# Sketched attention feeding a squared-ReLU network on one core: compact q features, planned order of the engines and a shorter prologue

## The chip, the core and the metric

The kernel runs on one core of one Trainium2 chip. The metric is the device time of that core in microseconds (us), median of several executions. A core has four compute engines that matter here: PE multiplies matrices (its weight loads are listed apart as PEld), DVE works elementwise and shuffles or transposes inside blocks of 32 rows, ACT copies and applies functions, POOL does small setup work and copies. SP only issues transfers.

## The reference, cut to what matters

```python
batch, n_heads, seq, head_dim = (4, 4, 1088, 32)         # float32
r = 8                                                   # rows of S1 and S2

def phi(x):                                             # 8 x 8 = 64 features per head
    a = np.einsum('rd,bhsd->bhsr', S1, x)
    b = np.einsum('rd,bhsd->bhsr', S2, x)
    return np.einsum('bhsi,bhsj->bhsij', a, b).reshape(*x.shape[:-1], r * r)
q_p, k_p = (phi(q), phi(k))
kv  = np.einsum('bhsf,bhsd->bhfd', k_p, v)
z   = np.sum(k_p, axis=2)
num = np.einsum('bhsf,bhfd->bhsd', q_p, kv)
den = np.einsum('bhsf,bhf->bhs', q_p, z)[..., None] + 1e-06
x   = (num / den) as 4352 rows of 128                   # 4 batches x 1088 rows, 4 heads x 32
h   = np.maximum(x @ w_in, 0.0)                         # w_in  128 x 2048
out = h * h @ w_out                                     # w_out 2048 x 128
```

Both kernels cut a batch into three chunks of at most 384 rows (384, 384, 320), and the 2048 hidden columns into 16 steps of 128. One FFN step is one f16 matmul `pg` (x times `w_in`), a Relu on ACT, a square, and one float32 matmul `po` (the square times `w_out`). There are 4 x 3 x 16 = 192 such steps.

## The kernel before

The q features need, for 4 heads x 64 features = 256 products, both factors spread over 256 rows. The kernel before lets PE do the spreading: the weights `sqa` and `sqb` hold each row of S1 and S2 eight times over. A matmul uses only 64 rows of the array, those of two heads, so there are two of each kind per group of columns:

```python
for c0 in range(0, S, 512):
    for pr in range(2):
        pa = psa.tile([128, 512], F32, tag="feat")
        nc.tensor.matmul(pa[:, 0:n], sqa[64*pr : 64*pr+64, :], qT[64*pr : 64*pr+64, c0 : c0+n])
        sa = wpool.tile([128, 512], F32, tag="sa")
        nc.scalar.copy(sa[:, 0:n], pa[:, 0:n])
        pb = psa.tile([128, 512], F32, tag="feat")
        nc.tensor.matmul(pb[:, 0:n], sqb[64*pr : 64*pr+64, :], qT[64*pr : 64*pr+64, c0 : c0+n])
        nc.vector.tensor_tensor(out=qp[...], in0=pb[:, 0:n], in1=sa[:, 0:n], op=mult)
    yield
```

The other matmuls of attention are `kf` (k features), `kvp` (k features times v with a column of ones) and `nd` (q features times `kvp`: numerator and denominator). The main loop runs all of batch 0's attention first, then the FFN of each batch with a stage of the next batch's attention at every fourth step. The order of instructions on each engine is left to a scheduler, which sees this program order:

```python
att = attn_gen(0)
for i, _ in enumerate(att): ...                  # the whole attention of batch 0
for b in range(B):
    issue_loads(b + 1); nxt = attn_gen(b + 1)    # (if there is a next batch)
    for t0, t1 in CHUNKS:
        for i, _ in enumerate(ffn_gen(b, t0, t1)):   # pg, Relu, square, po of one step
            if i % 4 == 2:
                next(nxt, None)
```

Of the kernel before, what the change touches and what calls it, by code (L numbers as in the profile page):

```python
# [9 lines left out]
F32 = mybir.dt.float32  # L10
# [10 lines left out]

@with_exitstack
def kernel(
# [13 lines left out]
    B, H, S, D = 4, 4, 1088, 32  # L37
    G = S // 32
    DFF = 2048
    NFF = DFF // 128  # L40
    NT = (S + 127) // 128
    TW = [min(128, S - 128 * t) for t in range(NT)]
    CHUNKS = [(0, 3), (3, 6), (6, 9)]
# [5 lines left out]
    Relu = mybir.ActivationFunctionType.Relu  # L49
    Copy = mybir.ActivationFunctionType.Copy  # L50
# [4 lines left out]
    fpool = ctx.enter_context(tc.tile_pool(name="ffn", bufs=4))  # L55
    psf = ctx.enter_context(tc.tile_pool(name="psf", bufs=3, space=bass.MemoryType.PSUM))
    psa = ctx.enter_context(tc.tile_pool(name="psa", bufs=2, space=bass.MemoryType.PSUM))


    s_nat = cpool.tile([128, 32], F32)  # L60
    nc.gpsimd.memset(s_nat[:], 0.0)
    for h in range(H):
        nc.sync.dma_start(s_nat[32 * h : 32 * h + 8, :], S1[:, :])
        nc.scalar.dma_start(s_nat[32 * h + 8 : 32 * h + 16, :], S2[:, :])

    def load_qk(dst, src, b, eng):
        eng.dma_start(
            dst[:, :],
            bass.AP(src.tensor, src.offset + b * H * S * D, [[G * D, 128], [1, G * D]]),
        )  # L70

    def load_v(dst, b):

        for g4 in range(4):
            for h in range(H):
                n = (G - g4 + 3) // 4
                nc.sync.dma_start(
                    _ap(dst, 32 * g4, 32, 33 * h, [[4 * 33, n], [1, 32]]),
                    bass.AP(
                        v.tensor,  # L80
                        v.offset + ((b * H + h) * S + g4) * D,
                        [[G * D, 32], [4 * D, n], [1, D]],
                    ),
                )

    loaded = {}

    def issue_loads(b):
        kn = bpool.tile([128, S], F32, tag="kn")
        qn = bpool.tile([128, S], F32, tag="qn")  # L90
        va = bpool.tile([128, NT * H * 33], F32, tag="va")
        load_qk(kn, k, b, nc.sync)
        nc.gpsimd.memset(_ap(va, 0, 128, 32, [[33, NT * H]]), 1.0)
        load_v(va, b)
        load_qk(qn, q, b, nc.scalar if b == 0 else nc.sync)
        loaded[b] = (kn, qn, va)

    issue_loads(0)

    w_in32 = cpool.tile([128, DFF], F32)  # L100
    nc.sync.dma_start(w_in32[:], moe_w_in[:, :])
    w_in = cpool.tile([128, DFF], F16)
    w_o = cpool.tile([128, DFF], F32)
    nc.sync.dma_start(
        _ap(w_o, 0, 128, 0, [[128, NFF], [1, 128]]),
        bass.AP(
            moe_w_out.tensor, moe_w_out.offset, [[128, 128], [128 * 128, NFF], [1, 128]]
        ),
    )

    iden = cpool.tile([128, 128], F32)
    make_identity(nc, iden[:])
    iden16 = cpool.tile([128, 128], F16)
    nc.gpsimd.tensor_copy(iden16[:], iden[:])

    s_T = cpool.tile([128, 32], F32)
    nc.vector.transpose(s_T[:, :], s_nat[:, :])
    sk = cpool.tile([128, 64], F32)
    sqa = cpool.tile([128, 128], F32)
    sqb = cpool.tile([128, 128], F32)  # L120
    nc.gpsimd.memset(sk[:], 0.0)
    nc.gpsimd.memset(sqa[:], 0.0)
    nc.gpsimd.memset(sqb[:], 0.0)
    for h in range(H):
        nc.vector.tensor_copy(  # L125
            sk[32 * h : 32 * h + 32, 16 * h : 16 * h + 16], s_T[32 * h : 32 * h + 32, 0:16]
        )
    for h in range(H):
        c = 64 * (h % 2)
        nc.vector.tensor_copy(  # L130
            _ap(sqa, 32 * h, 32, c, [[8, 8], [1, 8]]),
            _ap(s_T, 32 * h, 32, 0, [[1, 8], [0, 8]]),
        )
        nc.vector.tensor_copy(
            _ap(sqb, 32 * h, 32, c, [[8, 8], [1, 8]]),
            _ap(s_T, 32 * h, 32, 8, [[0, 8], [1, 8]]),
        )


    kvs = []  # L140
    for i in range(2):
        kv = cpool.tile([128, 2 * 66], F32, tag=f"kv{i}")
        nc.gpsimd.memset(kv[:], 0.0)
        kvs.append(kv)

    xT = {}
    betas = {}

    def attn_gen(b):
        kn, qn, va = loaded[b]  # L150
        kT = bpool.tile([128, S], F32, tag="kT", bufs=1)
        qT = bpool.tile([128, S], F32, tag="qT", bufs=1)
        qp = bpool.tile([128, 2 * S], F32, tag="qp", bufs=2)
        kv_sb = kvs[b % 2]
        xTb = bpool.tile([128, S], F16, tag="xT")
        beta = bpool.tile([128, NT], F32, tag="beta")
        xT[b], betas[b] = xTb, beta
        for c0, c1 in ((0, 512), (512, S)):
            nc.vector.transpose(kT[:, c0:c1], kn[:, c0:c1])  # L159
        yield  # L160
        for c0, c1 in ((0, 512), (512, S)):
            nc.vector.transpose(qT[:, c0:c1], qn[:, c0:c1])  # L162
        yield

        kvp = psa.tile([128, 2 * 66], F32, tag="acc", bufs=1)
        for t0 in range(0, NT, 3):
            kf = psa.tile([128, 3 * 64], F32, tag="feat")
            for i in range(3):
                w = TW[t0 + i]
                nc.tensor.matmul(  # L170
                    kf[0:w, 64 * i : 64 * i + 64],
                    kT[:, 128 * (t0 + i) : 128 * (t0 + i) + w],
                    sk[:, :],
                )
            fb = wpool.tile([128, 3 * 32], F32, tag="fb")
            kp = wpool.tile([128, 3 * 256], F32, tag="kp")
            segs = [(128, 3)] if TW[t0 + 2] == 128 else [(128, 2), (TW[t0 + 2], 1)]
            i0 = 0
            for w, n in segs:
                nc.scalar.copy(  # L180
                    _ap(fb, 0, w, 32 * i0, [[8, 4 * n], [1, 8]]),
                    _ap(kf, 0, w, 64 * i0 + 8, [[16, 4 * n], [1, 8]]),
                )
                i0 += n
            for i in range(3):
                w = TW[t0 + i]
                nc.vector.tensor_tensor(  # L187
                    out=_ap(kp, 0, w, 256 * i, [[64, 4], [8, 8], [1, 8]]),
                    in0=_ap(kf, 0, w, 64 * i, [[16, 4], [1, 8], [0, 8]]),
                    in1=_ap(fb, 0, w, 32 * i, [[8, 4], [0, 8], [1, 8]]),  # L190
                    op=mult,
                )
            for i in range(3):
                t = t0 + i
                w = TW[t]
                for pr in range(2):
                    nc.tensor.matmul(  # L197
                        kvp[:, 66 * pr : 66 * pr + 66],
                        _ap(kp, 0, w, 256 * i + 128 * pr, [[1, 128]]),
                        _ap(va, 0, w, t * H * 33 + 66 * pr, [[1, 66]]),  # L200
                        start=(t == 0 and pr == 0),
                        stop=(t == NT - 1),
                        skip_group_check=True,
                    )
            yield
        for h2 in range(2):
            nc.scalar.copy(
                _ap(kv_sb, 64 * h2, 64, 33 * h2, [[66, 2], [1, 33]]),
                _ap(kvp, 64 * h2, 64, 33 * h2, [[66, 2], [1, 33]]),
            )  # L210

        for c0 in range(0, S, 512):
            n = min(512, S - c0)
            pas, pbs = [], []
            for pr in range(2):
                pa = psa.tile([128, 512], F32, tag="feat")
                nc.tensor.matmul(  # L217
                    pa[:, 0:n], sqa[64 * pr : 64 * pr + 64, :], qT[64 * pr : 64 * pr + 64, c0 : c0 + n]
                )
                pas.append(pa)  # L220
                sa = wpool.tile([128, 512], F32, tag="sa")
                nc.scalar.copy(sa[:, 0:n], pa[:, 0:n])  # L222
                pb = psa.tile([128, 512], F32, tag="feat")
                nc.tensor.matmul(  # L224
                    pb[:, 0:n], sqb[64 * pr : 64 * pr + 64, :], qT[64 * pr : 64 * pr + 64, c0 : c0 + n]
                )
                nc.vector.tensor_tensor(  # L227
                    out=qp[:, pr * S + c0 : pr * S + c0 + n],
                    in0=pb[:, 0:n],
                    in1=sa[:, 0:n],  # L230
                    op=mult,
                )
            yield

        for t0, t1 in CHUNKS:
            nd = psa.tile([128, 3 * 132], F32, tag="acc", bufs=1)
            for t in range(t0, t1):
                w = TW[t]
                for pr in range(2):
                    o = 132 * (t - t0) + 66 * pr  # L240
# [162 lines left out]
```

## Time and profile before

Median 288.25 us of three runs (287.9 to 290.56); profiled span 286.6 us. I cut the span where ACT starts copying the last chunk of a batch out of `po` (tile `oT`), because at that point the batch's last `po` matmul is done.

| Stage | us | PE busy in it |
|---|---|---|
| start to first `pg` matmul | 53.29 | 37.9 |
| first `pg` to the end of batch 0 | 64.49 | 64.1 |
| batch 1 | 59.38 | 58.4 |
| batch 2 | 59.59 | 58.2 |
| batch 3 (FFN alone) | 43.53 | 41.4 |
| output of the last chunk | 6.32 | 0.6 |

The first fence is from the profile page of the kernel before: busy time with the share of the span and the number of instructions; the busy tenths of PE and the granted PE clock in 40 equal slices; the chain of waits by engine; two groups of instructions (busy us, mean ns, then idle time before them and what ended it).

```profile
PE 260.4 (91%) x1104; PEld 157.9 (55%) x1104; DVE 153.9 (54%) x441; ACT 114.2 (40%) x302; POOL 2.2 (1%) x17
...
PE   0578996999999999999989999999899999999991
...
PEclk9999999999999999999999999999999999999997
...
PE 86%; DVE 4%; ACT 3%; DMA 3%; issue 2%; ACTq 0%; DVEq 0%
...
L224 PE MATMUL pb<-qT,sqb 64*128 64x512 f32 (+1 forms) x48 | 25.2, 610 | 3.7 <-DVE qp L227 2.0
L217 PE MATMUL pa<-qT,sqa 64*128 64x512 f32 (+1 forms) x48 | 25.7, 621 | 0.9 <-DVE qp L227 0.9
```

PE is the limit: 91% busy, and 86% of the chain.

A float32 matmul is recorded as two passes ("x2"). In the prologue a pair `pa`, `sa`, `pb`, `qp` runs one after the other, 5.6 us from 14.86 to 20.45, and a `pa` takes 2.02 us where it takes 1.05 in the middle of the kernel. PE is at half speed there, although the clock row says 9 throughout.

### The profile page before, as it was taken

How to read it: one execution, taken by the hardware profiler on the slowest of the kernel's cores; microseconds unless marked ns; L12 is line 12 of the kernel's file. 1: busy time of each engine (PE TensorE's matmuls, PEld its weight loads, DVE VectorE, ACT ScalarE, POOL GpSimd, SP SyncE). 2: the span in 40 equal slices, each digit the busy share in tenths (PEclk: the TensorE clock that was granted, in tenths of full speed). 3: DMA queues.
4: the chain of work that ended last, by engine and by line, in shares of the span. 5: the costliest groups of instructions: out<-in, count | busy, mean ns of one | idle time of the engine just before them, and what ended most of it. 6: DMA issues, size and time to landing. Idle time of an engine off the chain costs nothing.

```text
span 286.6 us, 3493 instructions
## 1 busy us (share of the span) xinstructions
PE 260.4 (91%) x1104; PEld 157.9 (55%) x1104; DVE 153.9 (54%) x441; ACT 114.2 (40%) x302; POOL 2.2 (1%) x17
## 2 busy tenths in 40 slices
PE   0578996999999999999989999999899999999991
PEld 0422765856743578677434687765346664444550
DVE  0810106569634587937346788655345784653550
ACT  0211040423534363546434645436344445463541
POOL 2000000000000000000000000000000000000000
PEclk9999999999999999999999999999999999999997
DMA  4486520000037022000000000000000000000000
GB/s 156 64 285 155 177 41 8 0 0 0 3 77 199 0 57 70 0 25 1 27 0 0 26 4 1 24 1 29 0 0 3 27 1 22 3 29 0 22 6 23
DMA packets 24889, 11.23 MB, mean 39 GB/s; under 512 B 18856, under 2 KB 23208, under 8 KB 24744
## 3 DMA queue, kind: packets, MB, share of 16 engines
q1 hardware_dynamic: 24664, 10.46, 14.1%
q10 hardware_dynamic: 208, 0.56, 0.5%
q8 instruction: 8, 0.13, 0.2%
q14 instruction: 9, 0.07, 0.1%
HBM read 8.79 MB, written 2.23 MB: 38 GB/s over the span
## 4 chain that ended last, share of the span: by engine, by line
PE 86%; DVE 4%; ACT 3%; DMA 3%; issue 2%; ACTq 0%; DVEq 0%
PE po L322 43%; PE pg L315 10%; PE pb L224 7%; PE kvp L197 7%; PE nd L241 7%; PE pa L217 6%; PE kf L170 4%; ACT gt L320 2%; DMA kn<-in_k_dram 2%; PE op L337 2%; DVE qp L227 1%; PE xp L300 1%; ACT oT L331 0%; ACT sa L222 0%; DMA s_nat<-in_S_dram 0%
## 5 line engine op out<-in xcount | busy, mean ns | idle before, releaser
L320 ACT ACTIVATE gt<-pg 128x384 f32<-128x384 f32 (+1 forms) x192 | 78.2, 480 | 70.3 <-PE pg L315 68.2
L315 PE MATMUL pg<-xTb,w_in 128*128 128x384 f16 (+1 forms) x192 | 47.4, 323 | 2.6 <-ACT gt L320 2.1
L315 PEld LDWEIGHTS <-w_in 128*128 128x128 f16 x192 | 19.6, 107 | 23.1 <-issue 15.3
L227 DVE TENSOR_TENSOR qp<-pb,sa 128x512 f32<-128x512 f32 (+1 forms) x24 | 12.7, 531 | 34.6 <-PE pb L224 24.7
L224 PE MATMUL pb<-qT,sqb 64*128 64x512 f32 (+1 forms) x48 | 25.2, 610 | 3.7 <-DVE qp L227 2.0
L217 PE MATMUL pa<-qT,sqa 64*128 64x512 f32 (+1 forms) x48 | 25.7, 621 | 0.9 <-DVE qp L227 0.9
L197 PEld LDWEIGHTS kvp<-va,kp 128*128 128x128 f32 (+1 forms) x144 | 22.0, 225 | 6.3 <-issue 5.5
L222 ACT COPY sa<-pa 128x512 f32<-128x512 f32 (+1 forms) x24 | 11.1, 461 | 35.3 <-PE pa L217 33.1
L170 PE MATMUL kf<-sk,kT 128*128 128x64 f32 (+1 forms) x72 | 13.8, 334 | 12.4 <-DVE sk L125 10.3
L197 PE MATMUL kvp<-va,kp 128*128 128x66 f32 (+1 forms) x144 | 23.1, 309 | 0.0
L241 PE MATMUL nd<-kv,qp 128*128 128x66 f32 (+1 forms) x144 | 22.1, 294 | 0.0
L241 PEld LDWEIGHTS nd<-kv,qp 128*128 128x128 f32 (+1 forms) x144 | 20.2, 208 | 2.8 <-issue 1.5
L170 PEld LDWEIGHTS kf<-sk,kT 128*128 128x128 f32 (+1 forms) x72 | 12.9, 250 | 13.9 <-issue 13.1
L224 PEld LDWEIGHTS pb<-qT,sqb 64*128 64x128 f32 x48 | 8.6, 217 | 15.4 <-DVE qp L227 5.5
L187 DVE TENSOR_TENSOR kp<-kf,fb 128x256 f32<-128x256 f32 (+1 forms) x36 | 13.2, 411 | 6.4 <-PE kvp L197 5.1
L217 PEld LDWEIGHTS pa<-qT,sqa 64*128 64x128 f32 x48 | 8.3, 215 | 8.6 <-issue 5.6
L306 ACT COPY xTb<-xp 128x384 f16<-128x384 f16 (+1 forms) x12 | 5.5, 462 | 16.5 <-PE xp L300 16.1
L341 ACT ACTIVATE ob<-op,beta 128x128 f32<-128x128 f32 (+1 forms) x36 | 10.7, 379 | 2.9 <-PE op L337 2.9
L331 ACT COPY oT<-po 128x384 f32<-128x384 f32 (+1 forms) x12 | 5.5, 462 | 15.4 <-PE po L322 15.4
L258 DVE TENSOR_SCALAR den<-nd 128x12 f32<-128x12 f32 (+2 forms) x16 | 2.6, 161 | 16.3 <-PE nd L241 16.3
L159 DVE STREAM_TRANSPOSE kT<-kn 128x512 f32<-128x512 f32 (+1 forms) x8 | 5.6, 721 | 6.6 <-DMA kn<-in_k_dram 6.6
L162 DVE STREAM_TRANSPOSE qT<-qn 128x512 f32<-128x512 f32 (+1 forms) x8 | 5.6, 722 | 3.8 <-PE pb L224 3.8
(640 smaller groups left out, 387.2 us busy)
## 6 DMA issues: line engine op xcount, KB each, us to landing
kn<-in_k_dram SPq DMA_DIRECT2D x4, 544.0 KB
out_dram<-ob SPq DMA_DIRECT2D x32, 64.0 KB
qn<-in_q_dram SPq DMA_DIRECT2D x3, 544.0 KB
va<-in_v_dram SPq DMA_DIRECT2D x32, 36.0 KB
va<-in_v_dram SPq DMA_DIRECT2D x32, 32.0 KB
w_in_105<-in_moe_w_in_dram SPq DMA_DIRECT2D x1, 1024.0 KB
qn<-in_q_dram ACTq DMA_DIRECT2D x1, 544.0 KB
out_dram<-ob SPq DMA_DIRECT2D x4, 32.0 KB
```

The costliest lines, as they stand in the source:

```text
L170: nc.tensor.matmul(kf[0:w, 64 * i : 64 * i + 64], kT[:, 128 * (t0 + i) : 128 * (t0 + i) + w], sk[:, :],)
L187: nc.vector.tensor_tensor(out=_ap(kp, 0, w, 256 * i, [[64, 4], [8, 8], [1, 8]]), in0=_ap(kf, 0, w, 64 * i, [[16, 4], [1, 8], [0, 8]]), in1 ...
L197: nc.tensor.matmul(kvp[:, 66 * pr : 66 * pr + 66], _ap(kp, 0, w, 256 * i + 128 * pr, [[1, 128]]), _ap(va, 0, w, t * H * 33 + 66 * pr, [[1, ...
L217: nc.tensor.matmul(pa[:, 0:n], sqa[64 * pr : 64 * pr + 64, :], qT[64 * pr : 64 * pr + 64, c0 : c0 + n])
L222: nc.scalar.copy(sa[:, 0:n], pa[:, 0:n])
L224: nc.tensor.matmul(pb[:, 0:n], sqb[64 * pr : 64 * pr + 64, :], qT[64 * pr : 64 * pr + 64, c0 : c0 + n])
L227: nc.vector.tensor_tensor(out=qp[:, pr * S + c0 : pr * S + c0 + n], in0=pb[:, 0:n], in1=sa[:, 0:n], op=mult,)
L241: nc.tensor.matmul(nd[0:w, o : o + 66], qp[:, pr * S + 128 * t : pr * S + 128 * t + w], kv_sb[:, 66 * pr : 66 * pr + 66],)
L315: nc.tensor.matmul(pg[:, 0:n], w_in[:, 128 * c : 128 * c + 128], xT[b][:, c0 : c0 + n])
L320: nc.scalar.activation(gt[:, 0:n], pg[:, 0:n], Relu)
L322: nc.tensor.matmul(po[:, 0:n], w_o[:, 128 * c : 128 * c + 128], g2[:, 0:n], start=(c == 0), stop=(c == NFF - 1),)
L341: nc.scalar.activation(ob[0:w, o : o + 128], op[0:w, o : o + 128], Copy, bias=0.0, scale=betas[b][0:w, t : t + 1],)
```

## The change

Its intent is to take work from PE in the middle, to start the FFN earlier, and to fix the order of every engine by a plan:

1. **Compact q features.** One matmul `qc` gives the 16 projections of each head once (64 of 128 rows used, one 32-row block per head). DVE shuffles rows inside the 32-row blocks to make the factors: one shuffle for `qb`, two for `qa`. So 256 features become two halves of all four heads, `kvp` and `nd` become 132 columns wide instead of 66, and a mask takes out products across heads.
2. **Order.** The scheduler is switched off. A small planner assigns each attention task to an FFN step, from a table of durations. The `pg` of a step is issued 3 steps ahead of its `po`. A square goes to ACT when the plan has ACT less loaded than DVE (76 of 192, the number by which ACT's instructions differ in the experiment squares_dve; I had counted 78 beforehand; none of them in the last batch, which has no attention to plan for).
3. **Short prologue.** Only batch 0's first chunk is made before the FFN. Its q features use replicated weights (three matmuls `rep`, no shuffles). Loads come in parts, `kf` of all tiles goes first, 8 idle matmuls keep PE active while the first x is made.

The diff replaces nearly the whole body. Its core, with cuts:

```diff
+    ctx.enter_context(tc.manual_schedule())
...
-                    kvp[:, 66 * pr : 66 * pr + 66],
-                    _ap(kp, 0, w, 256 * i + 128 * pr, [[1, 128]]),
-                    _ap(va, 0, w, t * H * 33 + 66 * pr, [[1, 66]]),
...
+                kvp[:, 132 * e : 132 * e + 132],
+                kp[:, 256 * (t % 4) + 128 * e : 256 * (t % 4) + 128 * e + 128],
+                va[b % 2][:, 132 * t : 132 * t + 132],
...
+            out=kvz[:, :], in0=st[b, "kvp"][:, 0 : E * 132], in1=hmask[:, :], op=mult
...
-                nc.tensor.matmul(
-                    pa[:, 0:n], sqa[64 * pr : 64 * pr + 64, :], qT[64 * pr : 64 * pr + 64, c0 : c0 + n]
-                )
...
+        nc.tensor.matmul(qc[:, 0:384], sq[:, :], qT[:, 384 * ch : 384 * ch + 384])
...
+        nc.vector.stream_shuffle(in_=st[b, "qc", ch][:, 0:384], out=qb[:, :], mask=mask_b)
...
+        nc.vector.stream_shuffle(in_=st[b, "qc", ch][:, 0:384], out=qa[:, :], mask=mask_a[e])
...
+        if sq_on_act:
+            nc.scalar.activation(g2[:, 0:n], gt[:, 0:n], Square)
+        else:
+            nc.vector.tensor_tensor(out=g2[:, 0:n], in0=gt[:, 0:n], in1=gt[:, 0:n], op=mult)
...
+    P = _Plan(NS + 4, {"PE": 0.95, "DVE": 1.2, "ACT": 0.6, "POOL": 9.0, "SP": 9.0})
...
+    for i in range(NS + 4):
+        if i + LA < NS:
+            ffn1(i + LA, act_square(i + LA))     # pg, Relu, square, LA = 3 steps ahead
+        if i < NS:
+            ffn2(i)                              # po
+        for f, args in P.slots[i]:               # the attention tasks planned for this step
+            f(*args)
```

(The comments are mine. `e` counts the two halves of the features, `b` batches, `ch` chunks.)

## The prediction

> **What bounds the kernel now.** The page: span 286.6 us (timed median 288.25), PE busy 91%, DVE 54%, ACT 40%; 86% of the chain of waits is PE. The timeline and the chain show three stages.
>
> 1. Prologue, 0 to 53.3 us, where the first `pg` matmul starts. PE waits for loads and batch-0 features, and its passes run at half speed: `kvp` takes 0.22 us a pass at 28 us, 0.108 at 183 us. The PEclk row shows 9 throughout, so it hides this. The Trainium skill ("TensorE: Matmul & The Clock Gate", Part 1) describes such a cold clock; the trace agrees.
> 2. Middle: the chain repeats every 59.38 us per batch (88.55, 147.93, 207.31), PE 98% busy: PE throughput.
> 3. Last batch, 232 to 280.3 us: 48.3 us for FFN alone, worth 38.4 by the steps below: `po` waits for DVE squares, `pg` for ACT Relus: latency, from issue order.
>
> **PE cost, start to start in the timeline.** FFN step: `po` 0.646 + `pg` 0.163 = 0.81 us (0.68 at 320 columns): 36.75 us per batch, unchanged. Kv and nd matmuls become 132 columns wide instead of 66, but at 0.108 us a pass they look weight-load-bound (an f16 load measures 107 ns); I estimate 0.113 us a pass, 4.1 us each group, nearly free. `pa`+`pb` (about 8.5 us per batch: 1.05 and 0.86 us per two passes of 512 columns, plus the rests) become three 384-column `qc`, 1.95 us: 6.5 us saved. Period: 36.75 + kf 2 + kv 4.1 + qc 1.95 + nd 4.1 + transposes 2.1 = 51 us.
>
> **DVE and ACT.** Added: nine shuffles per batch. The skill ("VectorE: DVE Perf Modes", perf-mode tier table) gives the shuffle only the 1x program; the 128x512 transpose takes 0.69 us here, so I estimate 0.55 us for 384 columns. No shuffle is in this trace. 78 of 192 squares go to ACT (about 0.45 us each). Summing the planned tasks at traced durations over the FFN part: PE 194.5 us, DVE 123, ACT 128, and PE is largest in every group of eight steps. So PE stays the limit; the added DVE work is off the critical path.
>
> **Prologue after.** Estimate: k half lands at 4 us, kf 5.5 (cold, 0.5 each) to 10, rep to 12.5, kv to 17 or 20 (warm or cold), kvz, nd to about 21, small DVE chain 2.4, transposes and copy 1.2: first `pg` at 24.5 us. The rest of batch 0 (4 us of PE) moves into FFN.
>
> **Sum.** 24.5 + 1 (fill) + 194.5 + 4 stalls + 5.5 tail = 229.5 span; plus 1.65 outside it and a little for the unexpected: 232 us, range 224 to 243. Sources: prologue about 25 us net, `pa`/`pb` 20, last batch 10.
>
> Chances: faster by over 2%: 0.98; within 2%: 0.01; slower: 0.01.
>
> **What would show it.** First `pg` at 22 to 28 us. Period 51 to 53 us. `qc` 0.65 us start to start; nd and kv passes at most 0.12 us; shuffles about 0.55 us. Last batch 38.5 us. DVE and ACT both near 60%.
>
> **What would make it wrong.** Kv/nd passes well over 0.113 us; hand order stalling PE because `po` or `nd` waits for DVE behind attention work; only two `pg` buffers with ACT doing Relu and square; PE cold through the prologue or re-throttled at its end; POOL copies holding up DVE; w_in landing late.

## More of the kernel before

`pa` and `pb` together have 51 us of busy time, but a mean over the span hides that they cost twice as much early as later. The chain in order of time (start, duration, what) shows the early ones:

```profile
14.86 2.02 PE pa L217 x2
...
16.89 0.59 ACT sa L222
...
17.62 2.05 PE pb L224 x2
...
19.70 0.70 DVE qp L227
...
20.45 2.08 PE pa L217 x2
...
28.12 5.74 PE kvp L197 x26
```

The stages, from the windows of the trace (stretch and length; then busy us and count of PE, PEld, DVE, ACT, POOL; granted clock; DMA share; GB/s):

```profile
0.00:53.29 53.29, 37.88 (x117) 25.09 (x118) 15.48 (x47) 8.09 (x17) 2.00 (x16) 1.00 0.45 119
...
117.78:177.16 59.38, 58.38 (x279) 36.17 (x277) 37.61 (x108) 27.59 (x75) 0.00 (x0) 1.00 0.04 10
...
236.75:280.28 43.53, 41.35 (x150) 22.05 (x148) 22.18 (x48) 21.30 (x58) 0.00 (x0) 1.00 0.05 13
```

In batch 1 PE has work 98% of the time and DVE 63%: a middle batch is paid in PE work. The last batch has no attention beside it and still takes 43.5 us.

## The result, and the profile after

The kernel after takes 227.03 us (median of 4 runs, 226.17 to 227.38) beside 288.62 us for the kernel before (4 runs, 287.9 to 290.56). The ratio is 0.7853, with a 95% interval of 0.7807 to 0.79. Here and below, a ratio is the mean time of one kernel's fast runs over the mean of the other's fast runs in the same rounds, so it is not quite the ratio of the medians quoted. The profiled execution is one of the four, 227.35 us, with a span of 225.6 us.

The page of the kernel after:

```profile
PE 209.5 (93%) x1044; PEld 144.0 (64%) x1044; DVE 142.0 (63%) x371; ACT 149.2 (66%) x359; POOL 12.2 (5%) x47
...
PE   0896899989999999999999999999999999999990
...
PEclk9999699999999999999999999999999999999996
...
PE 50%; issue 40%; ACT 3%; DVE 2%; DMA 1%; POOL 1%; POOLq 0%; ACTq 0%; DVEq 0%
...
L325 PE MATMUL nd<-kvz,qp 128*128 128x132 f32 x144 | 20.1, 277 | 0.6 <-DVE kvz L292 0.6
...
L309 DVE STREAM_SHUFFLE qa<-qc 128x384 f32<-128x384 f32 x22 | 11.9, 590 | 0.0
...
L299 PE MATMUL qc<-qT,sq 128*128 128x384 f32 x22 | 8.9, 486 | 0.0
```

PE lost 51 us of busy time and is still the fullest engine. `pa` and `pb`, 51 us, gave way to `qc`, 8.9 us (and 2 us of `rep`). The `nd` matmuls, twice as wide, take 20.1 us of busy time, less than the 22.1 they had, of which a part ran at half speed. Do not read the chain's "issue 40%" as a wait: the last output transfer is issued by POOL, which had nothing else to do for 89.7 us, and the chain follows that idle queue back. The chain's early part is sound:

```profile
6.66 3.98 PE kf L249 x18
10.64 1.97 PE rep L530 x6
12.60 4.06 PE kvp L281 x36
...
17.25 1.63 PE nd L325 x12
...
20.60 0.60 DVE sc L365
...
24.51 1.38 PE po L434 x2
...
29.13 0.65 PE po L434 x2
```

`kf` runs at 0.22 us a pass of 96 columns and `rep` right behind it at 0.33 us a pass of 384. In the middle 384 columns also take 0.33 us, so PE came to full speed within the first 4 us of its work. The stages from the windows, same columns as before:

```profile
0.00:22.74 22.74, 13.89 (x85) 11.68 (x86) 11.80 (x33) 6.62 (x14) 7.52 (x40) 1.00 0.81 229
22.74:80.52 57.78, 56.50 (x289) 39.52 (x289) 37.83 (x114) 42.38 (x101) 1.53 (x3) 0.97 0.14 41
80.52:131.55 51.03, 50.78 (x263) 35.33 (x262) 33.90 (x91) 37.66 (x93) 2.33 (x3) 1.00 0.15 45
131.55:181.83 50.28, 50.28 (x260) 35.32 (x259) 33.50 (x89) 37.33 (x91) 0.00 (x0) 1.00 0.04 12
181.83:218.95 37.12, 37.09 (x150) 21.76 (x148) 24.30 (x46) 24.11 (x57) 0.00 (x0) 1.00 0.05 16
...
22.74:28.30 5.56, 5.08 (x13) 2.50 (x13) 3.15 (x10) 4.18 (x9) 0.00 (x0) 0.69 0.12 46
```

Where the 61.0 us of span went (before minus after):

| Stage | before | after | gain |
|---|---|---|---|
| start to first `pg` | 53.29 | 22.74 | 30.6 |
| first `pg` to the end of batch 0 | 64.49 | 57.78 | 6.7 |
| batch 1 | 59.38 | 51.03 | 8.4 |
| batch 2 | 59.59 | 50.28 | 9.3 |
| batch 3 | 43.53 | 37.12 | 6.4 |
| output of the last chunk | 6.32 | 6.65 | -0.3 |

Batch 0's FFN stage gains less than the others because it took over the attention of chunks 1 and 2, about 4 us of PE by the prediction's estimate, and because PE's clock fell to 0.69 in its first 5.6 us (last line of the fence). A `po` matmul took 1.38 us there instead of 0.65.

How much PE time a batch needs, read from the PE timeline of a middle batch (from the start of each group of matmuls to the start of the next, summed by kind, us):

| | `po` | `pg` | `kf` | `kvp` | `nd` | q features | sum |
|---|---|---|---|---|---|---|---|
| before (117.78 to 177.16) | 30.98 | 7.71 | 1.81 | 4.12 | 3.99 | 8.75 | 57.4 |
| after (131.55 to 181.83) | 28.65 | 7.37 | 1.93 | 4.08 | 4.05 | 1.93 | 48.0 |

(The rest is small: transposes of about 1.6 us, and gaps.) So of some 9 us per batch, 6.8 come from the q features, and about 2.7 stand against `po` and `pg`. The latter is no less work. I put it down to waits that end in them and to what a change of array shape costs (see the experiments before_hand2 and before_hand3); it was not taken apart.

### The profile page after: what moved, and what is told of

Its sections match the earlier page's. It is cut to its first block, busy times and chain, and to the rows that moved or that the text cites. A ratio compares the mean times of both kernels' runs of the same rounds, so it can differ in the third digit from the quotient of the medians.

```text
span 225.6 us, 3224 instructions
## 1 busy us (share of the span) xinstructions
PE 209.5 (93%) x1044; PEld 144.0 (64%) x1044; DVE 142.0 (63%) x371; ACT 149.2 (66%) x359; POOL 12.2 (5%) x47
## 4 chain that ended last, share of the span: by engine, by line
PE 50%; issue 40%; ACT 3%; DVE 2%; DMA 1%; POOL 1%; POOLq 0%; ACTq 0%; DVEq 0%
PE po L434 24%; PE pg L415 7%; PE nd L325 6%; PE kvp L281 5%; PE kf L249 3%; PE qc L299 2%; ACT gt L422 1%; DMA s_nat<-in_S_dram 1%; PE op L453 1%; PE rep L530 1%; POOL sr L201 1%; PE xp L395 1%; ACT xT L404 1%; POOLq L681 0%; POOL va_116 L228 0%
## 5 line engine op out<-in xcount | busy, mean ns | idle before, releaser
L422 ACT ACTIVATE gt<-pg 128x384 f32<-128x384 f32 (+1 forms) x192 | 89.8, 470 | 49.5 <-PE pg L415 48.7
L415 PE MATMUL pg<-xT,w_in 128*128 128x384 f16 (+1 forms) x192 | 61.2, 319 | 1.0 <-ACT xT L404 0.6
L325 PEld LDWEIGHTS nd<-kvz,qp 128*128 128x128 f32 x144 | 19.6, 190 | 5.0 <-DVE kvz L292 0.8
L325 PE MATMUL nd<-kvz,qp 128*128 128x132 f32 x144 | 20.1, 277 | 0.6 <-DVE kvz L292 0.6
L249 PE MATMUL kf<-sk,kT 128*128 128x96 f32 x72 | 11.2, 306 | 6.7 <-POOL sr L201 6.7
L249 PEld LDWEIGHTS kf<-sk,kT 128*128 128x128 f32 x72 | 11.3, 225 | 9.0 <-POOL sr L201 6.6
L281 PEld LDWEIGHTS kvp<-va_116,kp 128*128 128x128 f32 x72 | 10.7, 190 | 4.2
L267 DVE TENSOR_TENSOR kp<-fs 128x1024 f32<-128x1024 f32 (+1 forms) x12 | 11.4, 953 | 2.4 <-ACT fs L260 2.4
L309 DVE STREAM_SHUFFLE qa<-qc 128x384 f32<-128x384 f32 x22 | 11.9, 590 | 0.0
L281 PE MATMUL kvp<-va_116,kp 128*128 128x132 f32 x72 | 11.1, 277 | 0.0
L281 PEld LDWEIGHTS kvp<-va_113,kp 128*128 128x128 f32 x72 | 9.6, 190 | 2.4
L281 PE MATMUL kvp<-va_113,kp 128*128 128x132 f32 x72 | 9.8, 276 | 0.0
```

The costliest lines, as they stand in the source:

```text
L249: nc.tensor.matmul(kf[:, 96 * i : 96 * i + 96], kT[:, 128 * (t0 + i) : 128 * (t0 + i) + 128], sk[:, :])
L267: nc.vector.tensor_tensor(out=_ap(kp, 0, 128, 0, [[32, 8 * n], [8, 4], [1, 8]]), in0=_ap(fs, 0, 128, 0, [[4, 8 * n], [1, 4], [0, 8]]), in1 ...
L281: nc.tensor.matmul(kvp[:, 132 * e : 132 * e + 132], kp[:, 256 * (t % 4) + 128 * e : 256 * (t % 4) + 128 * e + 128], va[b % 2][:, 132 * t : ...
L309: nc.vector.stream_shuffle(in_=st[b, "qc", ch][:, 0:384], out=qa[:, :], mask=mask_a[e])
L325: nc.tensor.matmul(nd[:, 132 * o : 132 * o + 132], st[b, "qp", ch, e][:, 128 * o : 128 * o + 128], st[b, "kvz"][:, 132 * e : 132 * e + 132 ...
L415: nc.tensor.matmul(pg[:, 0:n], w_in[:, 128 * c : 128 * c + 128], st[b, "xT"][:, 384 * ch : 384 * ch + n],)
```

## The experiments

My theory after the result: the gain is PE work taken away plus an earlier start, and the new DVE work lies in PE's shadow. The rivals: fixing the order by hand is itself worth most of the middle's gain; the shuffles on DVE hold PE back, so that replicated matmuls would do as well; the replicated first features and the idle matmuls are what makes the prologue short. An expectation states what each theory would give; where it names a theory by a letter or a short word, its numbers tell which of these is meant. All kernels gave correct results.

### auto_order: the same program with the scheduler on

```diff
-    ctx.enter_context(tc.manual_schedule())
```

> The changed kernel with the hand order switched off, so that the automatic scheduler may reorder (one line removed). Theory A (the gain is PE work and program structure; the emission order already holds the pipelining, and the compiled PE order hardly differs): within 1% of the changed kernel, 225 to 230 us. Rival B (the gain is the fixed order itself): at least 10 us longer, 237 us or more.

Measured: 224.73 us (224.11 to 225.44), ratio 0.7793 (0.7752 to 0.7833), a little under the 225 to 230 us of theory A. It is not slower than the kernel after; the medians differ by 2.3 us in its favour, and the intervals of the two ratios just overlap. Its first `pg` comes later (24.65 us), but the first chunk is done at 42.14 us instead of 44.23, since the scheduler placed more of chunk 1's attention ahead of the first `pg`. Batches 1, 2 and 3 are the same within 0.5 us (50.6, 50.3, 37.1). So switching the scheduler off is worth nothing; the program order that the planner writes is enough for it.

### before_hand: the old arithmetic in a hand order

The main loop is rewritten as the change has it: `pg` 3 steps ahead of `po`, one stage of attention after each step (with more, shorter stages), scheduler off.

```diff
+    ctx.enter_context(tc.manual_schedule())
+    LA = 3
...
+    for i in range(LA):
+        ffn1(i)
+    for i in range(NS):
...
+        if i + LA < NS:
+            ffn1(i + LA)
+        ffn2(i)
...
+        next(nxt, None)
```

> The kernel before, its arithmetic untouched, but ordered by hand: pg issued 3 steps ahead of po, one small attention stage after each FFN step, scheduler off. Theory A: the middle period falls only from 59.4 to 57.5-58.5 us (its PE work), the last batch from 43.5 to about 37.5 us; with the prologue about as long as before, 273 to 284 us in all. Rival B: most of the 61 us comes from order, 250 us or less.

Measured: 316.69 us (315.47 to 317.29), ratio 1.0975 (1.0918 to 1.1032). This is a plain miss: I expected a gain and got a loss of 28 us. The first `pg` came at 65.7 us (12.4 later than before), batches 1 and 2 took 65.6 and 68.5 us instead of 59.4 and 59.6; only the last batch became shorter, 39.1 instead of 43.5. A hand order of the old operations is not by itself an improvement. Why the middle lost 6 to 9 us is the subject of before_hand2 and before_hand3.

### before_compact: the new arithmetic alone

The kernel before, with its scheduler, its loads and its prologue, but with `qc`, shuffles, 132-column `kvp` and `nd`, and the mask.

```diff
-                    pa[:, 0:n], sqa[64 * pr : 64 * pr + 64, :], qT[64 * pr : 64 * pr + 64, c0 : c0 + n]
...
+            nc.tensor.matmul(qc[:, 0:n], sq[:, :], qT[:, c0 : c0 + n])
+            qb = wpool.tile([128, 512], F32, tag="qb")
+            nc.vector.stream_shuffle(in_=qc[:, 0:n], out=qb[:, 0:n], mask=mask_b)
+            for pr in range(E):
+                qa = wpool.tile([128, 512], F32, tag="sa")
+                nc.vector.stream_shuffle(in_=qc[:, 0:n], out=qa[:, 0:n], mask=mask_a[pr])
```

> The kernel before with only the compact q features: one qc matmul, shuffles, 132-wide kv and nd, mask; automatic order and old prologue kept. Theory A: middle period 59.4 minus 6.5 = about 53 us, first batch shorter by 5 to 12 us, total 255 to 265 us. Rival B: under 8 us gained, 280 us or more.

Measured: 254.44 us (253.11 to 255.91), ratio 0.8823 (0.876 to 0.8887), just under the 255 to 265 us expected. This one part of the change brings 33.8 of the 61 us. The stages:

| Stage | before | before_compact | after |
|---|---|---|---|
| start to first `pg` | 53.29 | 39.67 | 22.74 |
| first `pg` to the end of batch 0 | 64.49 | 58.13 | 57.78 |
| batch 1 | 59.38 | 52.76 | 51.03 |
| batch 2 | 59.59 | 53.23 | 50.28 |
| batch 3 | 43.53 | 43.65 | 37.12 |

The three stages with attention in them gain 6.4, 6.6 and 6.4 us, which is the 6.8 us of PE work from the table above. The surprise is the first row. The compact features shorten even the old prologue by 13.6 us, where the `pa`, `sa`, `pb`, `qp` pairs ran one at a time and at half speed. Part of it is PE's speed: here the 36 passes of `kvp` take 6.62 us, 0.184 a pass on average, so PE left half speed for a time in the prologue, while in the kernel before it stayed there until about 58 us (a `po` takes 1.28 us at 56.48 and 0.65 at 58.72). In the chain of before_compact, what is left of the prologue is issue of loads, a load of `kn`, and a single run of `kvp` (the last line is from PE's timeline):

```profile
7.62 0.45 SPq L77
8.11 0.46 SPq L77
...
16.13 7.35 DMA kn<-in_k_dram
23.48 0.67 PE qc L214 x2
24.16 6.62 PE kvp L200 x36
...
19.32 2.07 PE L214 MATMUL qc<-qT,sq 128*128 128x512 f32 x2 [2.07 <-DVE qa L219]
```

That load of `kn` belongs to batch 1, and `qc` of batch 0 does not read it, so I do not trust this link of the chain. In PE's timeline PE is idle for 2.07 us before the second `qc`, until DVE has made the factors from the first, and for 2.07 us again before the third (at 23.47 us), just after DVE's next shuffles. So here, unlike in the middle, the shuffles seem to hold PE up.

Line 77 issues the v loads, 16 for a batch, at 0.5 us from one issue to the next. The kernel after needs 10 transfers for v, and its `kvp` run starts at 12.60 us; that the number of transfers makes this difference is not shown. The last batch did not move at all: it has no q features.

### replicate_all: the same plan, but PE spreads the q features

Batches 1 to 3 use three replicated matmuls per chunk in place of `qc` and three shuffles. The planner's limit for PE had to be raised for it to find room.

```diff
-    P = _Plan(NS + 4, {"PE": 0.95, "DVE": 1.2, "ACT": 0.6, "POOL": 9.0, "SP": 9.0})
+    P = _Plan(NS + 4, {"PE": 1.2, "DVE": 1.2, "ACT": 0.6, "POOL": 9.0, "SP": 9.0})
...
+                P.add(("qr", b, ch), "PE", 0.65, after, r_q, b, ch, 2, first=first)
+                P.add(("qb", b, ch), "ACT", 0.46, [("qr", b, ch)], r_qb, b, ch)
...
+                    P.add(("qa", b, ch, e), "PE", 0.65, [prev], r_q, b, ch, e)
```

> The changed kernel with batches 1 to 3 using replicated-feature matmuls (3 of 0.646 us per chunk instead of 1) and no shuffles: PE work up 9 x 1.29 = 11.6 us, DVE down about 9 us. Theory A (PE is the limit, shuffles hidden): 11.6 us longer, 236 to 242 us. Rival C (the shuffles on DVE are what holds the PE): unchanged or shorter, 222 to 230 us.

Measured: 238.35 us (238.2 to 238.47), ratio 0.8264 (0.8218 to 0.831): 11.3 us more than the kernel after. The added PE work is 3 batches x 3 chunks x 2 matmuls x 0.65 us = 11.7 us. Nearly all of it shows, although DVE has 27 shuffles fewer. So PE work is paid in full, and the rival that the shuffles hold PE falls.

### squares_dve: no squares on ACT

```diff
-        return P.load["ACT"][s] + 0.47 + 0.41 < P.load["DVE"][s] + 0.46
+        return False
...
-        ffn1(i, i % 2 == 1)
+        ffn1(i, False)
```

> The changed kernel with all 192 squares on DVE, none on ACT. Summed at traced durations DVE rises from 123 to 157 us against 194.5 us of PE, but in some stretches (steps 34 to 46) DVE then exceeds PE. Theory A: 3 to 11 us longer per these stretches, 230 to 238 us. Rival: since DVE's total stays below PE's, no change (within 1 us).

Measured: 235.75 us (234.88 to 236.49), ratio 0.817 (0.8144 to 0.8196): 8.7 us more than the kernel after. The stages to the ends of batches 0, 1 and 2 grow by 2.9, 3.7 and 2.1 us, and the last batch not at all (37.1; none of its squares was on ACT before). DVE is only 73% busy over the span, so a mean would have called this free. It is not, since attention's DVE work comes in dense stretches. The waits of this kernel (engine and line waited on; us in total, times, longest):

```profile
PEld po L434 <- DVE g L426: 14.1, 62, 0.5
```

and of the kernel after, where the same weight loads wait for nothing that is recorded:

```profile
PEld po L434 <- issue: 13.9, 66, 0.5
```

### shuffles_twice: every shuffle done twice

```diff
-        nc.vector.stream_shuffle(in_=st[b, "qc", ch][:, 0:384], out=qb[:, :], mask=mask_b)
+        for _ in range(2):
+            nc.vector.stream_shuffle(in_=st[b, "qc", ch][:, 0:384], out=qb[:, :], mask=mask_b)
```

(The same for `qa`.)

> The changed kernel with every shuffle issued twice: about 17 us more DVE work, nothing else. Theory A (DVE is off the critical path): 1 to 5 us longer (the prologue one and a few crowded stretches), 227 to 232 us. Rival C (DVE on the path): 12 us longer or more.

Measured: 231.96 us (231.69 to 232.24), ratio 0.8045 (0.803 to 0.806): 4.9 us more, for 33 shuffles x 0.49 us = 16 us of DVE work (start to start, the same estimate as below). By stages: 2.8 us to the end of batch 0, 0.9 in each of batches 1 and 2. So the shuffles are mostly, not wholly, in PE's shadow: about 70% of that work costs nothing, and batch 0, where two chunks' attention is crowded into the first steps, has the least room. The prediction's "off the critical path" is right as a first reading, with that correction.

### first_compact: first chunk without the replicated features

```diff
-    rep = {}
-    for j_, pool, tag in ((2, psf, "po"), (0, psa, "feat"), (1, psa, "tr")):
-        rep[j_] = pool.tile([128, 512], F32, tag=tag, name="rep")
-        nc.tensor.matmul(rep[j_][:, 0:384], sr[:, 128 * j_ : 128 * j_ + 128], qT[:, 0:384])
+    a_qc(0, 0)
...
+    a_qb(0, 0)
     for e in range(E):
+        a_qa(0, 0, e)
+        a_qp(0, 0, e)
```

(The POOL copies that build the replicated weights go as well.)

> The changed kernel with the first chunk of batch 0 done like all others (one qc matmul, three shuffles) instead of three replicated-feature matmuls. In the trace PE is the engine that runs without a gap from the rep matmuls (10.5 us) through kv (16.7), so the replicated form costs 1.3 us of PE there: I expect the first pg 0 to 1.3 us earlier, total 0 to 1.5 us shorter. The intent of the change says it should be 1 to 2 us longer, because DVE then has 1.6 us of shuffles in its chain.

Measured: 225.94 us (225.07 to 227.24, 5 runs), ratio 0.7837 (0.7814 to 0.7861), against 0.7853 (0.7807 to 0.79) for the kernel after. The intervals overlap: replicating the first features gives nothing that I can measure. The first `pg` comes at 22.41 us instead of 22.74.

### warm_fill: more idle matmuls around the first x

The clock of the kernel after fell to 0.69 between 22.74 and 28.30 us, just after PE had waited for the first x. If idle time of PE caused this, more filling should prevent it.

```diff
-    WARM = 8
+    WARM = 14
...
+    more_warm(4)
...
         ffn1(i, i % 2 == 1)
+        if i > 0:
+            more_warm(2)
```

> The changed kernel with 14 instead of 8 dummy matmuls after the first nd and 8 more in the gaps up to the first po. The trace shows the clock down to 0.69 between 22.7 and 28.3 us, in some runs only. If the gaps cause it: all runs at a clock of 0.99 or more and 1 to 2 us shorter, 225 to 226 us. If not: same or a little longer.

Measured: 226.81 us (225.88 to 227.57, 5 runs), ratio 0.7865 (0.7843 to 0.7887), not different from the kernel after. In the profiled execution the clock stayed up (0.996 over the span) and the first chunk was done at 42.93 us instead of 44.23, but that execution is the fastest of the five. All five had clocks of 0.991 or more, as expected if gaps cause the dip, but they were not 1 to 2 us shorter. The four runs of the kernel after had clocks from 0.984 to 0.997 and times from 227.38 to 226.17 us, so the dip comes and goes without help. What causes it stays open (PE's longest idle time just before it was 1.03 us); by these times it is worth about 1 us.

The run explained one small thing by accident. In the kernel after, a tiny DVE operation `sc` takes 0.59 us. In the timeline (start, us, engine, line, operation, tiles, and in brackets the idle time before it and what ended it) it starts with a POOL copy:

```profile
20.55 0.62 POOL L223 COPY va_116<-vn 128x512 f32<-128x512 f32 x1 [11.80 <-DMA vn<-in_v_dram]
...
20.60 0.59 DVE L365 TENSOR_TENSOR sc<-rden,rm 128x12 f32<-128x12 f32 x1
```

In warm_fill the POOL copy starts at 20.75 us, after `sc`:

```profile
20.71 0.17 DVE L365 TENSOR_TENSOR sc<-rden,rm 128x12 f32<-128x12 f32 x1
```

The Trainium skill, in "SBUF — State Buffer", section "Who interferes with whom", says that a DVE operation with two inputs in SBUF contends with a GpSimd operation that reads SBUF, by an exclusive lock. The two traces agree: 0.59 us beside the copy, 0.17 without. This was among the prediction's risks ("POOL copies holding up DVE"); here it cost about 0.4 us of the prologue.

### before_hand2: why the hand order lost (1)

The first suspect was the DVE chain that turns `nd` into x: in before_hand it ran as one block. Here it is split into three stages, with two more stage breaks beside it (after the copies of the k features and after `nd`), and a batch's attention may start as soon as the one before is through.

```diff
                     axis=AX, op=amax, apply_absolute_value=True,
                 )
+                yield
                 nc.vector.tensor_tensor(
                     out=m1[0:w, 0 : 4 * n], in0=mx[0:w, 0 : 4 * n], in1=rden[0:w, 0 : 4 * n], op=mult,
                 )
...
+    nxt = chain(attn_gen(1), attn_gen(2), attn_gen(3))
```

> The kernel before, hand ordered again, now with the DVE normalisation chain cut into three pieces in different FFN steps and kp apart from its copies. Theory: the first hand order lost 6 to 9 us per batch because squares, and so po, waited in DVE's queue behind the 2.4 us chain of small operations; then the middle period falls from 65.6-68.5 to 57.5-60 us, the last batch stays near 39 us. Rival: something else in the hand order costs it, the period stays above 63 us. The prologue, in plain program order, stays as long as in the first hand order, so the total is judged by stages (about 290 to 305 us).

Measured: 304.85 us (304.09 to 305.76), ratio 1.0555 (1.0503 to 1.0607). Batches 1 and 2 take 63.45 and 63.78 us, not the 57.5 to 60 that I expected. These changes together gave back 2 to 5 us of the loss per batch, not all of it. In the PE timeline of this run PE is fed, yet slower:

```profile
226.18 0.81 PE L344 MATMUL po<-g,w_o 128*128 128x384 f32 x2
226.91 1.12 PE L230 MATMUL pb<-qT,sqb 64*128 64x512 f32 x2
227.97 0.34 PE L329 MATMUL pg<-xTb,w_in 128*128 128x384 f16 x1
```

From start to start a `pb` of 512 columns takes 1.06 us and a `po` before it 0.73, where the work alone is 0.86 and 0.65. The kernel before had something else at that place:

```profile
142.45 0.81 PE L322 MATMUL po<-g_1223,w_o 128*128 128x384 f32 x2
143.19 0.69 PE L224 MATMUL pb<-qT,sqb 64*128 64x512 f32 x1
143.19 0.69 PE L217 MATMUL pa<-qT,sqa 64*128 64x512 f32 x1
```

There a `pb` and the next `pa` start in the same moment. They use different halves of the array's rows (heads 0 and 1, heads 2 and 3), and the scheduler had put them together. A hand order that puts an FFN step between them loses the overlap, and PE changes to 64 rows and back 12 times in a batch instead of 8 (counted in the two timelines). Start to start, `pa` and `pb` take 9.9 us of a batch here and 8.75 in the kernel before, so this is only about 1.1 of the 4 us that a batch is still longer.

### before_hand3: why the hand order lost (2)

The same kernel, with `pa` and `pb` on all 128 rows (weights padded with zeros), so that the array never changes its shape for them:

```diff
-                    pa[:, 0:n], sqa[64 * pr : 64 * pr + 64, :], qT[64 * pr : 64 * pr + 64, c0 : c0 + n]
+                    pa[:, 0:n], sqa[:, 128 * pr : 128 * pr + 128], qT[:, c0 : c0 + n]
```

> The second hand-ordered kernel before, with pa and pb on all 128 rows (weights zero in the other half) instead of 64. Its trace shows PE fed without waits in the q stretch, but pa or pb takes 1.06 us there instead of the 0.86 that 512 columns need, and the po around it 0.73 instead of 0.646. Theory: changing between 64-row and 128-row matmuls costs about 0.2 us at pa or pb and 0.09 at each neighbour; with 128 rows everywhere pa and pb take 0.86 us, po next to them 0.65, and the middle period falls from 63.5 to 60-61.5 us. Rival (no cost of the change of row mode; DVE with all 192 squares holds it): the period stays at 63 to 64 us.

Measured: 290.23 us (289.93 to 290.77), ratio 1.0054 (0.9995 to 1.0114). Batches 1 and 2 take 59.85 and 60.18 us, inside the 60 to 61.5 expected or just under it. The same PE work at the same place:

```profile
154.36 0.81 PE L344 MATMUL po<-g,w_o 128*128 128x384 f32 x2
155.01 1.02 PE L230 MATMUL pb<-qT,sqb 128*128 128x512 f32 x2
155.87 0.33 PE L329 MATMUL pg<-xTb,w_in 128*128 128x384 f16 x1
```

Now `pb` takes 0.86 us and `po` 0.65. Twice the rows, and faster: 0.2 us less at each `pa` or `pb`, and 0.09 at the neighbour, once the shape no longer changes. Summed start to start over batch 1, `pa` and `pb` fall from 9.9 to 7.5 us and `po` from 31.5 to 30.4, nearly all of the 3.6 us; 7.5 is also less than the 8.75 of the kernel before with its overlaps. The Trainium skill, in "TensorEngine Tiling (Array Packing)", section "Tiling Modes", under Key Properties, says that switching the tiling mode drains TensorE, and that tiles work independently and can execute in parallel. The traces agree with both: 1.06 against 0.86 us for the first, though the drain itself is not recorded, and the two matmuls that start at 143.19 us for the second. (This run's granted clock was 0.964, because it read 0.50 from about 50 to 66 us, mostly before the first `pg` at 62.06; batches 1 and 2 ran at full clock.)

The pair of runs shows one thing more. Up to 33.3 us the PE timelines of before_hand2 and before_hand3 are nearly alike, with all passes at half speed. Then `pa` and `pb` come, on 64 rows in the one and on 128 in the other, and after them the first `nd` (the first line is from before_hand2, the second from before_hand3):

```profile
47.82 2.83 PE L247 MATMUL nd<-kv,qp 128*128 128x66 f32 x12
...
45.37 1.50 PE L247 MATMUL nd<-kv,qp 128*128 128x66 f32 x12
```

With 128 rows PE is at full speed by then; with 64 rows it stays at half speed until about 72 us, and its first `pg` comes at 65.8 instead of 62.06. So the 64-row `pa` and `pb` may be what keeps PE slow in the old prologue; these are two profiled executions, and no run tests it in the kernel before itself.

What remains of hand order on the old operations is then: nothing in the middle (59.9 against 59.4 us, with the padded weights), and 3.8 us in the last batch (39.8 against 43.5).

### best_f32: the two small gains together

Scheduler on, and first_compact.

```diff
-    ctx.enter_context(tc.manual_schedule())
...
+    a_qc(0, 0)
```

> The changed kernel with both small gains together: automatic order allowed (224.7 us alone against 227.0) and compact first features (225.9 alone). If they add: 222.5 to 224.5 us. If both win the same gap before the first po: 224.5 to 226 us.

Measured: 224.35 us (223.28 to 225.67, 6 runs), ratio 0.7778 (0.7744 to 0.7811). The interval does not reach 0.7853, the kernel after's own ratio, but overlaps that kernel's interval (0.7807 to 0.79) by a hair, and auto_order's (0.7752 to 0.7833) fully. It is the fastest version here that keeps float32, about 1% under the kernel after. Whether the two gains add is open.

### po_f16: what limits next

The `po` matmul is the largest item left: 28.65 of a batch's 50.3 us. Here its two inputs are f16 (scaled so that they fit: Relu by 1/64, `w_out` by 4096). This changes the precision, so it is a probe of the limit and not a fair replacement.

```diff
-        g2 = fpool.tile([128, 384], F32, tag="g2", name="g2")
-        nc.scalar.activation(gt[:, 0:n], pg[:, 0:n], Relu)
+        g2 = fpool.tile([128, 384], F16, tag="g2", name="g2")
+        nc.scalar.activation(gt[:, 0:n], pg[:, 0:n], Relu, scale=1.0 / 64.0)
...
-            w_o[:, 128 * c : 128 * c + 128],
+            w_o16[:, 128 * c : 128 * c + 128],
```

> The changed kernel with squares and w_o in f16 (scaled so that nothing overflows), so that po runs at the f16 rate: PE work falls from 194.5 to 107 us. This changes precision; it is run to show the bound. Theory A (f32 po on PE is the limit, ACT with 128 us and DVE with 123 us next): 160 to 185 us, ACT and DVE the busiest. Rival (waits between engines, not PE throughput, set the pace): 205 us or more.

Measured: 185.44 us (183.58 to 186.62, one slow run of four included; the median of the three fast ones is 185.29), ratio 0.6405 of fast runs (0.6366 to 0.6443), just outside the 160 to 185 expected. Its profiled execution fell in the slow state (clock 0.928), so I compare no small difference from it. Batch 2 in its windows, same columns as above:

```profile
114.94:153.95 39.01, 34.38 (x212) 23.58 (x211) 33.42 (x89) 35.35 (x93) 1.47 (x3) 0.94 0.10 30
```

About 22 us of PE work per batch should have gone (an estimate from the expectation's 194.5 and 107 us for four batches); PE's busy time fell by 15.9 us, at a clock of 0.94, and the batch became only 11.3 us shorter (50.28 to 39.01). ACT is now busy 35.35 of 39.01 us, PE 34.38 and DVE 33.42. So in the kernel after PE is the limit, but with less work on PE, ACT and DVE soon are. The Trainium skill, "FP8 and Floating Point Precision", "TensorE Precision Notes", says that true float32 takes four passes through the array; the kernel after agrees, with 0.646 us for a float32 `po` and 0.163 for an f16 `pg` of the same 384 columns.

## Why the prediction was right or wrong, point by point

The time was right: 232 us predicted with 224 to 243 as the range, 227.03 measured. Its terms against the profile:

| Term | predicted, us | measured, us |
|---|---|---|
| first `pg` | 24.5 | 22.74 |
| FFN part: fill 1 + PE 194.5 + stalls 4 | 199.5 | 196.21 (22.74 to 218.95) |
| tail | 5.5 | 6.65 |
| span | 229.5 | 225.6 |

- **What bounds the kernel: right.** The named sign was "PE stays the limit". PE is busy 194.65 of the 196.21 us (the sum of the four windows from 22.74 to 218.95); the prediction had summed the planned tasks to 194.5. The mis-sized term is the stalls: fill and stalls together were put at 5 us and came to 1.6. (Busy time counts the half-speed passes of the dip too, so that it meets 194.5 so closely is partly luck.)
- **PE costs: right.** `qc` takes 0.65 us from start to start. A `kvp` pass takes 4.06 / 36 = 0.113 us, the figure estimated for 132 columns; `nd` 1.63 / 12 = 0.136 in the prologue, over the 0.12 named, and 0.113 later (0.90 for 8). Period: 51.0 and 50.3 us, predicted 51 to 53; last batch 37.1, predicted 38.5.
- **DVE and ACT: right in size, slightly wrong in effect.** Shuffles are recorded at 0.59 us and repeat every 0.49 (starts at 29.01, 29.50 and 30.00), with 0.55 predicted. The basis was the skill's "VectorE: DVE Perf Modes", perf-mode tier table, which gives the shuffle the 1x mode alone; the mode is not recorded, so the trace confirms only roughly the duration estimated from it. Shares of 63% and 66% were predicted as "near 60%". That the added DVE work is wholly off the critical path is not so: doubling it cost 4.9 of 16 us.
- **The prologue: right in time.** First `pg` at 22.7 us, with 22 to 28 named. The cold clock was rightly read in the kernel before. The skill's "TensorE: Matmul & The Clock Gate", Part 1, gives some 3.4 us of activity until full speed; the kernel after agrees (about 4 us), the kernel before does not (half speed until about 58 us; see the last section).
- **The split of sources: wrong.** This is the step that failed, in the prediction's words: "Sources: prologue about 25 us net, `pa`/`pb` 20, last batch 10." Its 20 us for `pa`/`pb` is three batches at 6.5, and before_compact shows this in the FFN stages (6.4 + 6.6 + 6.4 = 19.4). But the arithmetic change alone brings 33.8 us, since 13.6 of it lies in the old prologue, where the prediction had named loads, batch-0 features and a cold clock but not that `pa`/`pb` themselves were the chain; its 25 us for the prologue hid this share. The three FFN stages with attention gain 24.4 us (6.7 + 8.4 + 9.3) in the kernel after, where 20 less the 4 moved into batch 0 had been allowed: against before_compact, batches 1 and 2 gain another 4.7 us, and batch 0 takes over those 4 us and is still no longer. The last batch gains 6.4 and not 10: the window "232 to 280.3" began 4.8 us before batch 2 ended at 236.75, so batch 2's tail was counted in it. The errors had opposite signs, and the sum survived them.
- **The risks named.** "hand order stalling PE" did not happen in the kernel after, but it did in before_hand, with 28 us lost. PE "re-throttled at its end" did happen, once, for 5.6 us. "POOL copies holding up DVE" happened at one place, for 0.4 us. "Kv/nd passes well over 0.113 us" did not happen (0.136 in the prologue at most).

How the gain divides, as the runs show it: 33.8 us compact q features; of the other 27 to 28 us, 17 lie before the first `pg` (39.67 to 22.74), 6.5 in the last batch, and 4.7 in batches 1 and 2. In the last batch the hand order of the old kernel gave 3.8 of the 6.5; the other 2.7 no run takes apart (no squares are on ACT there, so it is not these), but the traces show more than half of it: in before_hand3 the first `po` of each of the three chunks starts 0.5 to 0.6 us late, idle until ACT has copied `oT` out of the only `po` buffer; the kernel after has two such buffers and no such wait. In the middle the split squares are needed: without them batches 1 and 2 lose 3.7 and 2.1 us. The parts of the short prologue were not all taken apart: the replicated features are worth nothing and more idle matmuls nothing, while fewer and earlier loads, `kf` of all tiles at once and postponing chunks 1 and 2 were changed together in every run I have.

## What to carry to other kernels

When one engine is the limit, price a change by the start-to-start time of that engine's instructions in each stage, and price the same instructions again in the prologue, where they may run one at a time and at half speed: here more than a third of one operation's cost lay there. Work moved to an engine that is 63% busy on average is free only where the plan leaves it room locally: about 30% of the doubled shuffles showed, and 8.7 us of the squares put back on it. An order tuned by a scheduler can hold overlaps that a neat hand order destroys (matmuls on different halves of the rows, 8.75 against 9.9 us a batch here), so test the order apart from the arithmetic.

## What the Trainium skill lacked or had wrong

- "TensorE: Matmul & The Clock Gate", Part 1: it gives about 3.4 us of sustained activity until PE is warm. In the kernel before, PE worked without a break from 26.05 to 36.85 us and stayed at half speed (`kvp` 5.74 us for 26 passes, 0.22 a pass, where 0.108 is usual later); `nd` at 50.94 us still took 0.213 a pass. The granted clock read 1.00 in that stretch, and also over the half-speed `kf` of the kernel after (6.66 to 10.64 us). The page warns that the clock's trace events may be unreliable and that the clock was seen stuck at a quarter for over 50 us, but not that a window's clock of 1.00 can stand over passes at half rate. Why PE stayed slow is not shown; before_hand2 and before_hand3, which differ in the rows of `pa` and `pb` alone, came out at half and at full speed (12 passes of `nd` in 2.83 and 1.50 us).
- "TensorEngine Tiling (Array Packing)", Tiling Modes: it says that a change of mode drains TensorE but gives no cost. Here it was 0.2 us at a 512-column float32 matmul on 64 rows between matmuls on 128 rows (1.06 against 0.86), and 0.09 at the `po` beside it (0.73 against 0.65); a matmul on all rows with half of the weights zero was the faster choice.
- "VectorE: DVE Perf Modes", perf-mode tier table: it gives the shuffle at one size only, about 2400 ns for 2048 columns. For 128 rows and 384 float32 columns read from PSUM, the records show 0.59 us, and 0.49 from start to start when several follow one another; loading the mask is recorded at 0.01 us.
- "Perfetto Trace Analysis", Engine Utilization, first footnote: it halves the rate for FP32_LOW_HIGH. The float32 matmul here costs four times the f16 one (0.646 against 0.163 us for 384 columns), as "FP8 and Floating Point Precision" has it; the two pages do not say how they fit together. In the trace such a matmul is two recorded passes of 0.32 us, each twice the f16 time, which would fit both; that these are what the footnote means is not shown.
